# Batch 0's first q and k by two hardware DMA queues, v and w_in triggered anew, its second phase held back, and batch 1's x transposed by DMA

## The chip, the cores and the metric

The kernel runs on one core of one Trainium2 chip, in one launch. The time is device microseconds of that core, from start to end of an execution. The kernel before was timed three times (343.29, 343.39, 343.57: median 343.39 us). One more execution was profiled.

## The reference

Causal attention with 16 extra "beacon" keys and values per head, and behind it a feed-forward layer with a squared ReLU, all without residuals:

```python
B, H, S, Nb, D = 8, 8, 576, 16, 64
k_all = concat([beacon_k, k]); v_all = concat([beacon_v, v])       # 592 keys
scores = q @ k_all.T / sqrt(D)                                     # causal over the 576, beacons always seen
a = softmax(scores)
x = (a @ v_all).transpose(0, 2, 1, 3).reshape(B * S, H * D)        # 4608 tokens x 512
h = x @ w_in                                                       # 512 -> 2048
out = relu(h) ** 2 @ w_out                                         # 2048 -> 512
```

Inputs and output are fp32 in HBM; the kernel computes in bf16 with fp32 accumulation.

## The kernel before

All work is given as small operations to a planner (class `Order`, L89). It holds for each operation the engine, an assumed duration, the operations it depends on and a priority, plays the program through once while the kernel is built, and emits the instructions of every engine in the order that results. On the chip each engine then works through its own list in order and waits on semaphores. So a change of a priority, of an assumed duration or of a limit on PSUM banks moves instructions on all engines. `deps` and `sync` become waits on the chip where data or a buffer is shared (`sync` adds such a wait where nothing is shared); `behind` only shapes the list.

**Attention, per batch and pair of heads** (four pairs per batch, so 32 pairs in all):

- q and k must be transposed. For batches 0 to 2 (`NPE = 3`) this is done on TensorE: `add_strided` (L502) loads q and k with the token index split as 96 partitions x 6, by GpSimd DMAs (L513) that cast fp32 to bf16 on the way. In batch 0 there is one DMA for each pair and each of q and k, eight in all; in batches 1 and 2 one for two pairs. In batches 1 and 2 a copy on VectorE ("spin", L382) brings the two heads of a pair side by side, so that one transpose serves both (L547, 12 per pair); in batch 0 each head is transposed by itself into one half of the PSUM partitions (L550, 24 per pair). Two copies then write kT (VectorE) and qT (ScalarE or VectorE).
- From batch 3 on, q and k are loaded by SP into staging slots (`stg`, eight of them), cast on GpSimd, and transposed by DMA (L459).
- Scores are computed in strips of up to 496 columns (L665), exponentiated on ScalarE (L680), masked on VectorE (L695, L699), multiplied with v (L715), and normalised on VectorE (L730, L731) into `xn`. v is loaded by SP (batch 1: by GpSimd) into `stg` and cast.
- Batch 0 is split into two phases (`NSPLIT = 1`, `SPLIT`): queries 0 to 239 and 240 to 575. The first has one score strip per pair, the second three.

**From xn to the MLP.** The MLP needs x transposed (`xT`). For batches 0 and 1 (`NXPE = 2`) this is done on TensorE (`add_xt_pe`, transposes at L779, copies on ScalarE or VectorE); later batches use five DMA transposes on SP (`add_xt`, L762).

**MLP.** Nine chunks of 512 tokens (`add_chunk`): first layer L843 with relu (L860 on ScalarE, L862 on VectorE) and square (L869), second layer L880, copies to `osb`, stores by SP. Chunk 0 is cut at token 240, where the first phase of batch 0 ends; chunk 1 needs rows of batch 1.

**The order of loads at the start.** GpSimd issues batch 0's eight q/k loads, the triangle mask, the casts of the first two v tiles, then w_in in four quarters (L804), batch 1's q/k, batch 1's v and w_out in four quarters (L813). SP loads the beacon keys (L475), then waits for the first q (`sync`) before it loads batch 0's five v tiles (L426, L427); w_in's first quarter waits for the third v tile (`sync`); batch 2's v, next on SP, waits for the last quarter of w_out (`sync`).

PSUM has eight banks. Classes of operations have limits on how many they may hold: score strips 6 (`strip`), AV 4, MLP 4, transposes 2 (`tp`).

Of the kernel before, what the change touches and what calls it, by code (L numbers as in the profile page):

```python
# [9 lines left out]
FP32 = mybir.dt.float32  # L10
# [78 lines left out]
class Order:  # L89
# [6 lines left out]
    START = {"PE": 0.0, "ACT": 1.5, "DVE": 0.7, "POOL": 0.5, "SP": 0.0, "-": 0.0}  # L96
# [16 lines left out]
    def run(self):  # L113
# [19 lines left out]
        lanes = {"SP": [], "POOL": []}  # L133
# [6 lines left out]
        while events:  # L140
# [16 lines left out]
            while again:  # L157
                again = False
                for e in engines:
# [58 lines left out]
                    if op.dma:  # L218
                        dma_free = max(dma_free, now + (0.65 if e == "SP" else 0.55 + 0.4 * op.dma)) + op.dma
# [34 lines left out]
def kernel(  # L254
# [80 lines left out]
    def wait_for(later, first):  # L335
# [5 lines left out]
        limits={"strip": 6, "av": 4, "mlp": 4, "tp": 2},  # L341
# [7 lines left out]
    nc.scalar.activation(warm, warm, AF.Exp)  # L349
# [20 lines left out]
    ident_op = add("ident", "POOL", 0.6, lambda e: make_identity(nc, ident), prio=-199.8)  # L370
# [28 lines left out]
    NXPE = 2  # L399
# [11 lines left out]
    def add_load(b, x, c, prio, behind=[], sync=[]):  # L411
# [34 lines left out]
        if x != "v":  # L446
            if b < NPE + 2:
                deps += [zero_ops[b]]
            else:
# [3 lines left out]
                            prio=prio, deps=deps, give=ld)  # L453
# [14 lines left out]

    tpb_ops = {}
# [32 lines left out]
    def add_strided(b, prio):  # L502
# [6 lines left out]
        for pr in range(0, HP, step):  # L509
            h = slice(2 * pr, 2 * (pr + step))  # L510
            for n, (x, t, dst) in enumerate((("k", k, ks), ("q", q, qs))):
                def emit(e, t=t, dst=dst, h=h):
# [3 lines left out]
                        deps=free, dma=0.87 * step if b else 1.12)  # L516
# [4 lines left out]
        for pr in range(HP):  # L521
# [11 lines left out]
            if b:  # L533
                for x, t in (("k", ks), ("q", qs)):
                    def emit_spin(e, h=h, x=x, t=t, blocks=blocks):
                        copy_on(e, blocks[x].rearrange("p s (h d) -> p h s d", h=2), t[b % 2][:, h])

                    spin[x].append(add(f"spin{b}{x}{pr}", "DVE", 0.45, emit_spin, prio=prio + pr,
                                       deps=[loads[pr, x]] + spin[x][-1:] + ([tps[b - 1, 0]] if pr == 0 and b > 1 else [])))

            def emit_tp(e, pr=pr, h=h, box=box, blocks=blocks):
                pp = pair(box["t"]).bitcast(BF16)
                for half, at, x, t in ((1, Nb, "k", ks), (0, 0, "q", qs)):
                    for u in range(NS):
                        cols = slice(at + u * NP, at + (u + 1) * NP)
                        if b:
# [8 lines left out]
                     deps=([spin["k"][pr], spin["q"][pr]] if b else [loads[pr, "k"], loads[pr, "q"]]) + [ident_op] + busy,  # L555
                     take=("ps", "tp", [2]), mode="full" if b else "columns")
# [89 lines left out]
    def add_scores(pairs, n, sizes):  # L646
# [4 lines left out]
        for size in sizes:  # L651
# [7 lines left out]
            def emit_qk(e, group=group, box=box):  # L659
                for k, (x, _, (mms, _, _)) in enumerate(group):  # L660
                    st = pair(box["qk"], k)
                    for c, t0, t1, col in mms:
# [11 lines left out]
                     take=("ps", "strip", [2] * size), gate=owners[0].gate, mode="rows")  # L674
# [125 lines left out]
    def add_weights():  # L800
        for i in range(4):
# [5 lines left out]
            w_ops["in", i] = add(f"win{i}", "POOL", 1.3, emit, prio=-100 + i, sync=[v_loads[0][2]] if i == 0 else (),  # L807
                                 behind=[w_ops["in", i - 1]] if i else (), dma=2.6)
    def add_weights_out():
        for i in range(4):  # L810
# [5 lines left out]
            w_ops["out", i] = add(f"wout{i}", "POOL", 1.3, emit, prio=-90 + i, behind=[v_loads[1][4]] if i == 0 else [w_ops["out", i - 1]], dma=2.6)  # L816
# [103 lines left out]
    for b in range(B):  # L920
# [76 lines left out]
```

## Time and profile before

| | |
|---|---|
| median of three runs | 343.39 us |
| profiled execution | 342.96 us |
| its span | 341.1 us |
| TensorE (PE) busy | 325.8 us |
| ScalarE (ACT) busy | 199.9 us |
| VectorE (DVE) busy | 156.5 us |
| GpSimd (POOL) busy | 84.4 us |

How to read the rows that follow. A row of groups or of the timeline has the start, the duration, the engine, the source line, the operation, what it writes and reads with sizes, and in square brackets the idle time before it and who ended that. A row of the stage table has the stretch and its length, then for PE, PEld (weight loads), DVE, ACT and POOL the busy time and the number of instructions, then the granted TensorE clock (1.00 is full), the mean busy share of the 16 DMA engines (above 1 where transfers overlap) and GB/s moved. A row of a tile's or line's instructions has the shortest, middle and longest duration in ns. In the DMA view, the last number of a row is the median time from issue to landing in us; the size is that of the destination.

### The profile page before, as it was taken

Reading aid. Unit: us, or ns where it says so; the run is one execution under the profiler, and the core shown is the slowest. Engines: PE = TensorE matmul, PEld = TensorE weight load, DVE = VectorE, ACT = ScalarE, POOL = GpSimd, SP = SyncE. Lnnn points to the kernel's source line nnn. Section 1 sums busy time; section 2 is a strip of 40 time slices with the busy share of each in tenths; the row PEclk is TensorE's granted clock in tenths of the full one; section 3 lists DMA queues with packets and bytes.
Section 4 is the critical chain, followed back from the end, with each engine's and each line's share of the span. In section 5 each row is a group of like instructions: output and inputs, shape, how many; then the busy total and the mean of one; then the engine's idle time right before and its main releaser. Section 6 shows DMA issues by size and latency. Waiting matters only on the chain.

```text
span 341.1 us, 7065 instructions
## 1 busy us (share of the span) xinstructions
PE 325.8 (96%) x2844; PEld 177.1 (52%) x2884; DVE 156.5 (46%) x313; ACT 199.9 (59%) x311; POOL 84.4 (25%) x133
## 2 busy tenths in 40 slices
PE   3899999999999999999999999999999999999995
PEld 2568765545455535543556865435544444444442
DVE  5576974569533655247523862267404202301400
ACT  3977977497747775558454755597326326515611
POOL 8364730466350231504151522200000000000000
PEclk9969999999999999999999999999999999999999
DMA  7999999999997996999799989930051011011002
GB/s 96 190 184 204 220 205 215 224 230 208 211 180 163 198 222 110 205 240 241 144 200 224 239 143 211 251 73 1 2 131 63 0 61 63 0 61 63 0 28 95
DMA packets 137008, 49.45 MB, mean 145 GB/s; under 512 B 123344, under 2 KB 132048, under 8 KB 136976
## 3 DMA queue, kind: packets, MB, share of 16 engines
q1 hardware_dynamic: 127184, 40.02, 59.4%
q0 software_dynamic: 9792, 8.98, 16.4%
q8 instruction: 22, 0.36, 0.5%
q14 instruction: 10, 0.08, 0.1%
HBM read 37.22 MB, written 9.44 MB: 137 GB/s over the span
## 4 chain that ended last, share of the span: by engine, by line
PE 90%; DMA 3%; ACT 3%; DVE 1%; issue 1%; POOL 0%; DVEq 0%; ACTq 0%; POOLq 0%
PE ps L880 36%; PE ps L843 35%; PE ps L715 9%; PE ps L665 8%; DMA kT<-qk_area 2%; ACT pt L680 2%; DMA qk_area<-in_q_dram 1%; PE ps L547 1%; PE ps L779 1%; ACT qT L380 1%; PE ps L550 1%; DVE g L862 0%; DVE xn L731 0%; DVE g L869 0%; ACT osb L380 0%
## 5 line engine op out<-in xcount | busy, mean ns | idle before, releaser
L843 PE MATMUL ps<-xT,w_in 128*128 128x512 bf16 (+3 forms) x687 | 133.4, 340 | 1.2 <-DVE g L862 0.3
L880 PE MATMUL ps<-w_out,g 128*128 128x512 bf16 x553 | 128.1, 379 | 1.6 <-issue 0.6
L680 ACT ACTIVATE pt<-ps 128x832 bf16<-128x832 f32 (+4 forms) x128 | 102.9, 874 | 19.1 <-PE ps L665 19.0
L843 PEld LDWEIGHTS <-w_in 128*128 128x128 bf16 x704 | 65.3, 98 | 56.5 <-issue 7.2
L860 ACT ACTIVATE g<-ps 128x512 bf16<-128x512 f32 (+2 forms) x125 | 69.6, 557 | 39.1 <-PE ps L843 38.2
L869 DVE TENSOR_TENSOR g<-g 128x1024 bf16<-128x1024 bf16 (+2 forms) x80 | 53.2, 666 | 79.4 <-ACT g L860 78.2
L880 PEld LDWEIGHTS <-g 128*128 128x128 bf16 x576 | 53.9, 98 | 63.3 <-issue 2.5
L380 ACT COPY osb<-ps 128x512 f32<-128x512 f32 x36 | 21.2, 589 | 67.1 <-PE ps L880 65.7
L382 POOL CAST qk_area<-stg 128x512 bf16<-128x512 f32 (+2 forms) x50 | 33.3, 676 | 55.5 <-DMA stg<-in_k_dram 30.3
L695 DVE TENSOR_TENSOR pt<-pt,tri 128x1024 bf16<-128x1024 bf16 (+1 forms) x36 | 24.9, 694 | 36.5 <-ACT pt L680 36.5
L382 POOL CAST vb<-stg 128x512 bf16<-128x512 f32 (+1 forms) x37 | 25.3, 695 | 61.3 <-DMA stg<-in_v_dram 42.0
L715 PEld LDWEIGHTS <-pt 128*128 128x128 bf16 (+1 forms) x960 | 34.8, 99 | 7.4 <-issue 1.4
L715 PE MATMUL ps<-vb,pt 128*128 128x65 bf16 (+1 forms) x960 | 36.2, 196 | 0.9 <-ACT pt L680 0.7
L665 PE MATMUL ps<-qT,kT 64*128 64x80 bf16 (+6 forms) x400 | 34.3, 290 | 2.2 <-ACT pt L680 0.9
L862 DVE TENSOR_SCALAR g<-ps 128x512 bf16<-128x512 f32 (+2 forms) x35 | 21.8, 626 | 13.8 <-PE ps L843 13.6
L731 DVE TENSOR_TENSOR xn<-ps,rcp 128x640 bf16<-128x640 f32 (+2 forms) x36 | 27.0, 751 | 1.3
L665 PEld LDWEIGHTS <-kT 64*128 64x128 bf16 x400 | 14.2, 98 | 22.7 <-issue 17.5
L730 DVE RECIPROCAL rcp<-ps 128x10 f32<-128x10 f32 (+2 forms) x36 | 7.6, 211 | 33.2 <-PE ps L715 29.8
L380 ACT COPY qT<-ps 128x576 bf16<-128x576 bf16 x12 | 7.8, 653 | 8.2 <-PE ps L550 4.8
L382 DVE COPY kT<-ps 128x576 bf16<-128x576 bf16 x12 | 9.0, 751 | 2.3 <-PE ps L550 1.4
L699 DVE TENSOR_TENSOR pt<-pt,tri 80x160 bf16<-80x160 bf16 x32 | 9.0, 281 | 0.0
L380 ACT COPY xT<-ps 128x576 bf16<-128x576 bf16 (+2 forms) x8 | 4.2, 519 | 3.6 <-PE ps L779 3.6
(43 smaller groups left out, 69.3 us busy)
## 6 DMA issues: line engine op xcount, KB each, us to landing
out_dram<-osb SPq DMA_DIRECT2D x17, 512.0 KB, 3.3
stg<-in_v_dram SPq DMA_DIRECT2D x21, 256.0 KB, 5.4
stg<-in_q_dram SPq DMA_DIRECT2D x20, 256.0 KB, 5.4
stg<-in_k_dram SPq DMA_DIRECT2D x15, 256.0 KB, 4.4
w_in<-in_moe_w_in_dram POOLq DMA_DIRECT2D x4, 512.0 KB, 8.1
w_out<-in_moe_w_out_dram POOLq DMA_DIRECT2D x4, 512.0 KB, 10.8
stg<-in_v_dram SPq DMA_DIRECT2D x7, 224.0 KB, 4.2
qk_area<-in_k_dram POOLq DMA_DIRECT2D x4, 288.0 KB, 12.2
```

The lines of the kernel that those rows point to most:

```text
L380: nc.scalar.copy(dst, src)
L382: eng[e].tensor_copy(dst, src)
L665: nc.tensor.matmul(st[:, hj, col:col + t1 - t0], kT[x.b % 2][hp, x.pr, 128 * c:128 * c + 128], qT[x.b % 2][hp, x.pr, t0:t1], start=True, s ...
L680: nc.scalar.activation(pt[x.take_pt.held[0]][:, :, off:off + width], pair(box["qk"], k)[:, :, 0:width], AF.Exp, bias=0.0, scale=scale)
L695: nc.vector.tensor_tensor(out=d, in0=d, in1=tri[:, m0:m0 + m, :][:, None].to_broadcast([128, 2, m, 128]), op=ALU.min)
L715: nc.tensor.matmul(a[:, hj, (t - tl[0]) * (D + 1):(t - tl[0] + 1) * (D + 1)], P[0:rr, hj, o:o + 128], vb[b % 2][0:rr, c, h, :], start=(c = ...
L731: nc.vector.tensor_tensor(out=xn[b % 2].rearrange("p t (h d) -> p h t d", d=D)[:, 2 * pr:2 * pr + 2, tl[0]:tl[0] + nt], in0=a[:, :, :, 0:D ...
L843: nc.tensor.matmul(h[:, lo - spans[0][0]:hi - spans[0][0]], w_in_sb[:, mc, ft * 128:(ft + 1) * 128], xT[:, mc, lo % RING:lo % RING + hi - lo],
L860: nc.scalar.activation(dst, h, AF.Relu, bias=0.0, scale=1.0)
L862: nc.vector.tensor_scalar(out=dst, in0=h, scalar1=0.0, scalar2=None, op0=ALU.max)
L869: nc.vector.tensor_tensor(out=d, in0=d, in1=d, op=ALU.mult)
L880: nc.tensor.matmul(o, G[:, fc, ts * 128:(ts + 1) * 128], w_out_sb[:, fc, :], start=(fc == 0), stop=(fc == NFT - 1))
```

## The change

- The first pair's q and k of batch 0 are loaded as fp32 by two hardware queues, k on SP and q on ScalarE's, into memory borrowed from `g[1]` (`first`). Copies on VectorE or ScalarE cast and turn them (`spin`), so that this pair takes 12 transposes instead of 24. The remaining six q/k loads of batch 0 stay on GpSimd.
- The load of the exp table moves behind ScalarE's DMA issue; the identity's memset moves from GpSimd to VectorE.
- v of batch 0 waits for the third pair's q (`strided[0][HP - 2, "q"]`) instead of the first pair's; w_in waits for the second v tile instead of the third; batch 2's v no longer waits for w_out (`behind` in place of `sync`, which is an order of the planner and no wait on the chip).
- Casts of batch 0's v tiles 2 to 4 get a later priority.
- Score strips of batch 0's second phase get a class of PSUM banks of their own (`late`, at most 4), transposes may hold 4 banks instead of 2.
- Batch 1's x is transposed by DMA on SP (`NXPE = 1`).
- Assumed durations of the planner: loads of q/k in batch 0 0.76 us instead of 1.12, issue of weights 0.95 instead of 1.3, ScalarE ready at 0.

The built program's lists show what the planner makes of it. TensorE before: pair 0's transposes and first strip, pair 1's transposes, pair 0's second-phase strips, pair 2's transposes and so on; after: transposes of pair 0, transposes of pair 1, first strip of pair 0, transposes of pair 2, first strip of pair 1, transposes of pair 3, first strip of pair 2, then the first second-phase strips of pair 0, then the four AVs of the first phase with the transposes of their results and strips of pairs 0 and 1 between them, and the first MLP matmul before the second phase of pairs 2 and 3 and before any second-phase AV. Batch 1's attention is also placed further ahead: all its score strips but one come before the first second-layer matmul of chunk 0. From chunk 2's first layer on TensorE's list is the same as before. On SP the five DMA transposes of batch 1's x stand ahead of all of batch 3's loads but one, and batch 2's first three v tiles directly behind batch 0's v.

```diff
-    START = {"PE": 0.0, "ACT": 1.5, "DVE": 0.7, "POOL": 0.5, "SP": 0.0, "-": 0.0}
+    START = {"PE": 0.0, "ACT": 0.0, "DVE": 0.7, "POOL": 0.5, "SP": 0.0, "-": 0.0}
...
-        limits={"strip": 6, "av": 4, "mlp": 4, "tp": 2},
+        limits={"late": 4, "strip": 6, "av": 4, "mlp": 4, "tp": 4},
...
-    nc.scalar.activation(warm, warm, AF.Exp)
...
+    nc.vector.memset(ident, 0.0)
+    nc.vector.memset(bks, 0.0)
     nc.vector.memset(tri, BIG)
-    nc.vector.memset(bks, 0.0)
...
-    ident_op = add("ident", "POOL", 0.6, lambda e: make_identity(nc, ident), prio=-199.8)
+    ident_op = add("ident", "POOL", 0.3, lambda e: make_identity(nc, ident, nomemset=True), prio=-198.85)
...
-    NXPE = 2
+    NXPE = 1
...
         cast[b, x, c] = add(f"cast{b}{x}{c}", engs, {"DVE": 0.6, "POOL": 0.65}, emit_cast,
-                            prio=prio, deps=deps, give=ld)
+                            prio=prio + (900.0 if b == 0 and c > 1 else 0.0), deps=deps, give=ld)
...
+    first = {x: g[1][0:NP].rearrange("p f t -> p (f t)")[:, 1536 * i:1536 * (i + 1)].bitcast(FP32).rearrange(
+        "p (h s d) -> p h s d", h=2, s=NS) for i, x in enumerate("kq")}
...
+        if b == 0:
+            add("table", "ACT", 1.5, lambda e: nc.scalar.activation(warm, warm, AF.Exp), prio=prio)
+        for n, (x, t) in enumerate((("k", k), ("q", q)) if b == 0 else ()):
+            def emit(e, t=t, x=x):
+                queue = nc.sync if e == "SP" else nc.scalar
+                return [queue.dma_start(out=first[x], in_=t[0, 0:2].rearrange("h (p s) d -> p h s d", s=NS))]
+
+            loads[0, x] = add(f"sld{b}{x}0", "SP" if n == 0 else "ACT", 0.5, emit, prio=prio - 1 + 0.1 * n, dma=0.76)
-        for pr in range(0, HP, step):
+        for pr in range(1 if b == 0 else 0, HP, step):
...
-                        deps=free, dma=0.87 * step if b else 1.12)
+                        deps=free, dma=0.87 * step if b else 0.76)
...
-            if b:
+            turned = b > 0 or pr == 0
+            if turned:
                 for x, t in (("k", ks), ("q", qs)):
                     def emit_spin(e, h=h, x=x, t=t, blocks=blocks):
-                        copy_on(e, blocks[x].rearrange("p s (h d) -> p h s d", h=2), t[b % 2][:, h])
+                        copy_on(e, blocks[x].rearrange("p s (h d) -> p h s d", h=2), t[b % 2][:, h] if b else first[x])
...
-                     take=("ps", "strip", [2] * size), gate=owners[0].gate, mode="rows")
+                     take=("ps", "late" if b < NSPLIT and n else "strip", [2] * size), gate=owners[0].gate, mode="rows")
...
-            w_ops["in", i] = add(f"win{i}", "POOL", 1.3, emit, prio=-100 + i, sync=[v_loads[0][2]] if i == 0 else (),
+            w_ops["in", i] = add(f"win{i}", "POOL", 0.95, emit, prio=-100 + i, sync=[v_loads[0][1]] if i == 0 else (),
...
-                    sync = [strided[0][0, "q"]]
+                    sync = [strided[0][HP - 2, "q"]]
...
             elif b == 2 and n == 0:
-                sync = [w_ops["out", 3]]
+                behind = [w_ops["out", 3]]
```

More of the change, by code (lines that the diff above doesn't have):

```diff
@@ L132, in run @@
         dma_free = 0.0
-        lanes = {"SP": [], "POOL": []}
+        lanes = {"SP": [], "POOL": [], "ACT": []}
         events = [(t, 0, None, None) for t in sorted(set(free.values()) | {0.0})]
@@ L218, in run @@
                     if op.dma:
-                        dma_free = max(dma_free, now + (0.65 if e == "SP" else 0.55 + 0.4 * op.dma)) + op.dma
+                        dma_free = max(dma_free, now + (0.65 if e != "POOL" else 0.55 + 0.4 * op.dma)) + op.dma
                         seen = max(end, dma_free + 1.4)
@@ L554, in add_strided @@
             tp = add(f"tp{b}.{pr}", "PE", 0.55 if b else 1.0, emit_tp, prio=100.0 * (HP * b + pr) - 190,
-                     deps=([spin["k"][pr], spin["q"][pr]] if b else [loads[pr, "k"], loads[pr, "q"]]) + [ident_op] + busy,
-                     take=("ps", "tp", [2]), mode="full" if b else "columns")
+                     deps=([spin["k"][pr], spin["q"][pr]] if turned else [loads[pr, "k"], loads[pr, "q"]]) + [ident_op] + busy,
+                     take=("ps", "tp", [2]), mode="full" if turned else "columns")
             tps[b, pr] = tp
@@ L815, in emit @@
                     in_=moe_w_out.rearrange("(c p) f -> p c f", p=128)[:, i * n:(i + 1) * n, :])]
-            w_ops["out", i] = add(f"wout{i}", "POOL", 1.3, emit, prio=-90 + i, behind=[v_loads[1][4]] if i == 0 else [w_ops["out", i - 1]], dma=2.6)
+            w_ops["out", i] = add(f"wout{i}", "POOL", 0.95, emit, prio=-90 + i, behind=[v_loads[1][4]] if i == 0 else [w_ops["out", i - 1]], dma=2.6)
     def add_chunk(j):
```

9 lines of the change are left out of this document (5 added, 4 removed).

## The prediction

> **What bounds the kernel now.** I read the page first: its row of engines and its slices.
>
> ```profile
> PE 325.8 (96%) x2844; PEld 177.1 (52%) x2884; DVE 156.5 (46%) x313; ACT 199.9 (59%) x311; POOL 84.4 (25%) x133
> ...
> PE   3899999999999999999999999999999999999995
> ...
> DMA  7999999999997996999799989930051011011002
> ```
>
> TensorE is busy throughout, except in the first slices and at the very end. The table of stages says how much is missing where.
>
> ```profile
> 0.00:5.00 5.00, 0.79 (x16) 0.69 (x16) 3.65 (x21) 1.49 (x2) 3.76 (x11) 1.00 0.47 64
> 5.00:10.00 5.00, 3.33 (x54) 2.37 (x52) 1.83 (x3) 2.28 (x4) 3.06 (x8) 1.00 1.16 152
> ...
> 12.50:15.90 3.40, 2.21 (x46) 1.44 (x43) 1.63 (x3) 3.40 (x6) 1.49 (x3) 1.00 1.26 216
> 15.90:19.30 3.40, 2.99 (x32) 1.78 (x31) 3.19 (x11) 2.92 (x5) 3.40 (x6) 0.50 0.59 89
> 19.30:22.70 3.40, 3.05 (x46) 2.50 (x43) 2.16 (x9) 2.67 (x5) 2.56 (x5) 0.50 1.23 205
> ...
> 24.70:48.00 23.30, 22.54 (x279) 17.83 (x278) 19.99 (x50) 19.59 (x40) 13.62 (x19) 1.00 1.22 211
> ...
> 72.00:336.00 264.00, 261.45 (x2038) 133.09 (x2071) 108.99 (x186) 148.00 (x225) 50.56 (x76) 1.00 0.67 132
> ```
>
> From 24.7 us on TensorE lacks 0.8 us up to 48 and 1% of the rest: what is computed there cannot be hidden, only removed. Before 24.7 it is idle for about 8 us, and the DMA engines are full (share above 1) from 5 to 15.9 and again from 18: the start waits for data. So a change at the start is worth the sum of four things: when dense work begins, how much attention is then still owed, at which clock it runs, and what TensorE work disappears.
>
> The clock needs a second look. The granted clock reads 1.00 up to 15.9, 0.50 up to 22.7, then 1.00. The same 24 transposes of one pair say otherwise for the beginning:
>
> ```profile
> 10.23 1.17 PE L550 MATMUL ps<-ident,qk_area 96*64 96x96 bf16 x24
> ...
> 12.61 0.70 PE L550 MATMUL ps<-ident,qk_area 96*64 96x96 bf16 x24
> ```
>
> 1.17 against 0.70 us: the array is already slow before about 12.5, fast for 3.4 us, slow again for 6.8 us, and fast once the work is dense.
>
> The chain of the start:
>
> ```profile
> 5.18 0.63 POOL L513 DMA_DIRECT2D qk_area<-in_q_dram  x1
> ...
> 8.04 0.78 ACT L680 ACTIVATE pt<-ps 128x736 bf16<-128x736 f32 x1 [0.58 <-PE ps L665]
> ...
> 15.64 3.00 POOL L804 DMA_DIRECT2D w_in<-in_moe_w_in_dram  x4 [1.01 <-DMA stg<-in_v_dram]
> ...
> 24.29 0.35 PE L665 MATMUL ps<-qT,kT 64*128 64x336 bf16 x4
> ...
> 24.74 0.57 PE L843 MATMUL ps<-xT,w_in 128*128 128x240 bf16 x4
> ...
> 25.72 0.32 PE L779 MATMUL ps<-ident,xn 128*128 128x128 bf16 x3 [0.41 <-DVE xn L731]
> ...
> 26.70 0.90 PE L715 MATMUL ps<-vb,pt 128*128 128x65 bf16 x24
> ```
>
> The first exp starts at 8.04, w_in is asked for at 15.64 (after the third v tile), and the first MLP matmul, the start of dense work, runs at 24.74.
>
> **The change part by part.** First the loads of q and k. They take, from issue to landing (answers of the DMA view for one issue each: batch 0's first k, its third q, batch 0's first v tile, the first quarter of w_in, batch 1's first q and second k):
>
> ```profile
> qk_area<-in_k_dram POOLq DMA_DIRECT2D x1, 144.0 KB, 3.0
> ...
> qk_area<-in_q_dram POOLq DMA_DIRECT2D x1, 144.0 KB, 5.2
> ...
> stg<-in_v_dram SPq DMA_DIRECT2D x1, 224.0 KB, 6.5
> ...
> w_in<-in_moe_w_in_dram POOLq DMA_DIRECT2D x1, 512.0 KB, 5.5
> ...
> qk_area<-in_q_dram POOLq DMA_DIRECT2D x1, 288.0 KB, 12.7
> ...
> qk_area<-in_k_dram POOLq DMA_DIRECT2D x1, 288.0 KB, 13.5
> ```
>
> The first k was issued at 1.36 and landed at 4.4; the third q landed at 5.18 + 5.2 = 10.4: five loads later, 1.2 us each, the last of them beside v. The pair on the hardware queues can be issued at 0.8 us instead of 1.36 and 2.11. No such load is in the trace; its landing lies between 1.9 us (below, the 32 KB beacon on SP) and 5.4 us (page, 256 KB of v in the busy stage) after issue; I take 3.2 us, nearer the short one because nothing else runs yet: 4.0. ACT also spends its issue there, and its table load (1.28 us) then still ends by 2.8, before the data.
>
> ```profile
> 0.80 0.40 SPq L475 DMA_DIRECT2D stg<-in_beacon_k_dram  x1
> ...
> stg<-in_beacon_k_dram SPq DMA_DIRECT2D x1, 32.0 KB, 1.9
> ...
> 0.80 1.28 ACT L349 ACT_TABLE_LOAD   x1 [0.80 <-PEq L981]
> ...
> L382 DVE CAST vb<-stg x3: 429/514/637, 15.1 to 18.3; 128x512 bf16<-128x512 f32 x2, 80x512 bf16<-80x512 f32 x1
> ```
>
> The new fp32-to-bf16 turn copies have 768 columns; a cast of 512 takes 0.43 to 0.64, so 0.65 to 0.95 each, on DVE and ACT in parallel. They end near 5.0. But the order built for TensorE now puts the second pair's transposes, which wait for GpSimd's first two loads, ahead of the first score strip. Those are issued as early as the old first pair, yet share the engines with 576 KB of fp32: about 6.2. So the first exp starts near 8.0, as before: the pair's head start buys nothing by itself.
>
> The remaining four GpSimd loads at 1.1 us each (the 1.2 above without v) put the third q at 8.4, 2 us earlier, and the fourth at 10.6. v is now triggered by the third q instead of the first:
>
> ```profile
> 6.43 7.16 SPq L427 DMA_DIRECT2D stg<-in_v_dram  x5
> ...
> 14.02 0.62 POOL L382 CAST vb<-stg 128x512 bf16<-128x512 f32 x1 [0.37 <-DMA stg<-in_v_dram]
> ...
> 16.00:17.00 1.00, 0.78 (x8) 0.46 (x7) 0.96 (x4) 1.00 (x3) 1.00 (x2) 0.50 0.14 21
> 17.00:18.00 1.00, 0.92 (x11) 0.55 (x11) 0.97 (x4) 1.00 (x2) 1.00 (x3) 0.50 0.25 18
> ```
>
> The second v tile was cast at 14.02, 7.6 us after v's first issue; the first k of the kernel took 3.0, and one tile of v more takes about 1.2. Between 4.2 and 7.6 after the trigger I take 5.0, since only two other loads are left beside it: 13.4 instead of 13.9. w_in follows the second v tile instead of the third: 13.5 instead of 15.64, and its first quarter lands at 19.0 instead of 21.1. This also closes the hole of the last two rows, in which the DMA engines ran at a share of 0.14 and 0.25.
>
> The second phase (queries 240 and up) of batch 0 gets its own class of banks, and the order now runs all four first phases before most second ones. From the landed v (13.4) to the first MLP matmul the new order holds, one behind the other, a cast of 0.5, four short AVs, four norms, transposes, xT copies and four score strips. With the slow strips and AVs (0.5 each) that makes 6.5 us, with fast ones (0.35) 4.7. Start of dense work: between 19.0 (w_in) and 19.9; I take **19.4, 5.3 us earlier than 24.7**.
>
> What is still owed then: before, one AV group and two groups of transposes were behind the first MLP matmul; now three more AV groups (0.90 each), two more transposes (0.32) and six score strips (0.35 alone, half of that in a stream, so 0.27): 2.7 + 0.6 + 1.6 = **4.9 us more**.
>
> The clock: TensorE in the changed order is sparse from 12 to 19.4 and so slow at 19.4. If it comes back at 22.7 as now, 3.3 us of dense work run at 0.70/1.17 of full rate: **1.3 us lost**.
>
> Batch 1's xT by DMA transposes removes 20 matmuls of TensorE and four ACT copies of 0.64 us.
>
> ```profile
> 40.00:75.00 35.00, 1.69 (x20) 1.44 (x20) 1.00 1.16 219
> ...
> L762 SPq DMA_TRANSPOSE xT<-xn x30: 1186/1264/2203, 96.8 to 251.9; - x30
> ...
> 68.74 1.90 PE L843 MATMUL ps<-xT,w_in 128*128 128x512 bf16 x8
> ...
> 61.80 5.65 SPq L427 DMA_DIRECT2D stg<-in_q_dram  x4
> ...
> 77.89 4.20 SPq L459 DMA_TRANSPOSE qT<-qk_area  x1
> ```
>
> The first row is these transposes alone: **1.7 us gone**. Their cover: the five DMA transposes take 5 times 1.3 to 2.2 us on SP after the last norm of batch 1 and must be there when chunk 1 begins (68.74 now). In the new order ten groups of four second-layer matmuls (the last row has eight of the first layer in 1.90) and four groups of transposes (0.70) stand between, about 12 us against 7 to 11. If that cover is gone, it costs up to 3 us. Batch 3's q, behind them on SP, moves from 61.80 to about 67; its own transposes are issued at 77.89 now, and TensorE has chunks 1 and 2 to work on until they land: nothing, and up to 5 us if the gap closes.
>
> The last edit drops batch 2's wait for w_out:
>
> ```profile
> SPq L426 <- DMA w_out<-in_moe_w_out_dram: 37.8, 1, 37.8
> ```
>
> Three v tiles (768 KB) that now go at 51 will go as soon as their slots are free, near 17 to 20, beside w_in and batch 1's q and k: bounded by nothing (they overlap) and 768 KB at the 205 GB/s of 19.3 to 22.7, 3.7 us of delay. Batch 1's second k now lands at 20.47 + 13.5 = 34.0; 2.1 us of earlier trigger and half of the delay nearly cancel, so I take zero here. The memsets moved to DVE, the planner's constants and the casts put behind cost nothing that the v wait does not hide.
>
> Sum: -5.3 + 4.9 + 1.3 - 1.7 = **-0.8 us**. The profiled execution took 342.96 (span 341.1 and 1.9 around it), the median is 0.4 above it; the forecast is 343.39 - 0.8 = **342.6**.
>
> **Rivals.**
>
> *Loads at their later speed (faster).* Batch 1's second k landed 1.5 us after its first q (19.80 + 12.7 and 20.47 + 13.5): 0.75 us for each 144 KB, not 1.1. The two to the third q then save 0.7 us, the first four together 1.4, and with less in front of v 1.8; dense work begins at 17.6: 340.8. For it: the slow figure was taken with v alongside. Against: the loads of 4.4 to 9 us, without v, were no faster.
>
> *Dropped wait (slower).* The 768 KB go ahead of w_in's last quarter and batch 1's q and k, which come 3.7 - 2.1 = 1.6 us later than now, while TensorE reaches them no later than now. The copies that turn them stand in DVE's queue ahead of norms and squares, and DVE has no room there (19.99 of 23.3 us now, and the new order gives it six more relus of 0.4 and the four late norms and masks): 1.6 us of waiting, and the squares behind it hold up TensorE for as long again, so 343.4 - 0.8 + 3.2 = 345.8, and 344.6 where 1.2 us of it is hidden, which I take. It decides as soon as batch 1's second k lands after about 36 (34.0 now).
>
> *One more slow stretch.* If the sparse start keeps the array slow for another 3.4 us, that loses 1.4 us more: 344.0, no measurable change. For it: after 15.9 the array needed two such stretches, though it was busy 2.99 of 3.40 us in the first. By the Trainium skill (TensorE: Matmul & The Clock Gate, "What's actually happening") the gate looks at free-running windows of 3.4 us; the trace agrees, 15.9 to 22.7 being two of them.
>
> *The change doesn't do what it says.* The two hardware loads only split one stream, and w_in is not earlier: dense work at 20.4 and 343.6. The Trainium skill (DMA: Bandwidth & Descriptors, "Issuing engines are not separate DMA queues") says that all issuing engines feed the same 16 DMA engines and that a second one saves only issue time; the share of 0.47 in the first 5 us leaves idle engines to fill, so the trace supports it only from 5 us on.
>
> **How the numbers follow.** Forecast 0.37 (its own range 341.8 to 343.3), faster loads 0.18, dropped wait 0.28, slow stretch 0.10, no earlier w_in 0.07. 0.2% is 0.69 us and about what can be told from no change: faster is below 342.7, slower above 344.1. Faster: 0.24 of the forecast and 0.18, together 0.42; slower: 0.27, 0.04 of the slow stretch and 0.03 of the last, 0.34; same: the rest, 0.24. The range takes in 340.8 less a little and the dropped wait with most of its 345.8: 340.4 to 345.4.
>
> **What would show it.** Right: the first MLP matmul between 19.0 and 19.9, w_in's issue near 13.5, the third q landed near 8.4, the first exp near 8, 1.69 us less under the transposes of xn, the granted clock at 1.00 from about 22.7. The dropped wait shows as waits of DVE's or TensorE's on qk_area or w_in between 25 and 40, and as more than 0.8 us of idle TensorE from there to 48. Wrong altogether: dense work after 21, or chunk 1's first matmul waiting for xT's DMA.

## The result, and the profile after

The changed kernel takes 349.44 us (median of four; the kernel before, beside it, 343.48): 1.016 times as long, 95% interval 1.0131 to 1.0189. The forecast was 342.6, and the time lies outside its range. The profiled execution took 349.52 us, its span 347.8. The changed file has 12 lines more ahead of the code in question, so L843 of before is L855, L665 is L677, L715 is L727, L762 is L774. The experiments' own additions move lines by up to 12 more.

The page of the changed kernel, engines and slices:

```profile
PE 327.2 (94%) x2813; PEld 177.1 (51%) x2852; DVE 160.8 (46%) x324; ACT 194.9 (56%) x300; POOL 81.9 (24%) x129
...
PE   2887999999999979999999999999999999999995
...
PEclk9969899999999999999999999999999999999999
```

TensorE has 31 matmuls fewer in the records and is yet 1.4 us longer busy: some of its work ran at a lower clock. Each matmul has a weight load of its own (PEld; in e8 below, whose records are complete, there are 2884 of each), so about 40 matmul records are missing both here (2813 against 2852) and before (2844 against 2884); idle times of the two can be compared with each other, but each is somewhat too long. Idle time is 20.6 us (347.8 less 327.2), 5.3 more than before. The stage table says where:

```profile
15.90:19.30 3.40, 2.47 (x27) 1.05 (x26) 2.43 (x10) 3.31 (x5) 3.33 (x6) 0.65 1.11 178
19.30:22.70 3.40, 2.53 (x19) 1.53 (x20) 1.40 (x5) 1.57 (x4) 0.67 (x1) 0.50 1.23 201
22.70:24.70 2.00, 2.00 (x49) 1.88 (x46) 1.19 (x4) 0.23 (x1) 0.54 (x1) 0.74 1.21 195
24.70:48.00 23.30, 21.15 (x256) 15.99 (x252) 18.21 (x48) 17.43 (x32) 12.80 (x18) 0.93 1.21 204
72.00:336.00 264.00, 259.42 (x2032) 132.29 (x2066) 111.59 (x189) 149.68 (x226) 48.34 (x74) 1.00 0.68 139
...
34.00:36.00 2.00, 2.00 (x29) 1.82 (x28) 1.55 (x6) 0.37 (x1) 1.23 (x3) 0.50 1.27 191
36.00:38.00 2.00, 2.00 (x22) 1.65 (x20) 0.88 (x3) 1.03 (x3) 0.89 (x2) 0.65 1.27 218
```

Two stretches that were dense are dense no longer. From 24.7 to 48 us 2.15 us are idle instead of 0.8, and the clock is 0.93 on average instead of 1.00; the last two rows show it at 0.50 and 0.65 just after a stall. From 72 us on 4.6 us are idle instead of 2.6. (The rest of the 5.3 is 1.35 more up to 24.7 us and 0.4 from 48 to 72.) The list of TensorE's waits names both (us in total, times, longest):

```profile
PE ps L677 <- DMA kT<-qk_area: 2.3, 2, 2.1
PE ps L490 <- DMA bks<-in_beacon_k_dram: 2.0, 1, 2.0
PE ps L855 <- DMA w_in<-in_moe_w_in_dram: 1.6, 1, 1.6
```

The third row is the start of dense work. Here is that start in the timeline:

```profile
9.02 5.41 SPq L427 DMA_DIRECT2D stg<-in_v_dram  x5
9.39 0.79 ACT L692 ACTIVATE pt<-ps 128x736 bf16<-128x736 f32 x1
...
13.68 3.00 POOL L816 DMA_DIRECT2D w_in<-in_moe_w_in_dram  x4 [0.71 <-DMA stg<-in_v_dram]
...
20.17 0.98 PE L855 MATMUL ps<-xT,w_in 128*128 128x240 bf16 x4 [1.63 <-DMA w_in<-in_moe_w_in_dram]
```

Dense work begins at 20.17 instead of 24.74: this half of the forecast came about, nearly as sized (4.6 us earlier, not 5.3). What follows did not. The first stall is for batch 1's beacon keys, `bks`, at 31 us:

```profile
17.43 6.75 SPq L427 DMA_DIRECT2D stg<-in_v_dram  x3
...
33.42 0.26 PE L490 MATMUL ps<-ident,bks 128*128 128x16 bf16 x4 [1.98 <-DMA bks<-in_beacon_k_dram]
...
33.71 0.23 DVE L494 CAST kT<-ps 128x64 bf16<-128x64 f32 x1 [2.10 <-PE ps L490]
33.85 0.45 DVE L382 COPY sparek<-qk_area 96x768 bf16<-96x768 bf16 x1
```

VectorE's queue stood behind it for 2.10 us, the copies that turn batch 1's first keys with it. `bks` is 16 KB and was issued at 17.31; it took this long (answers of the DMA view for one issue each, first before, then after: `bks`, batch 1's second k, first quarter of w_in; last `bks` in experiment e1, the changed kernel with the wait put back):

```profile
bks<-in_beacon_k_dram POOLq DMA_DIRECT2D x1, 16.0 KB, 11.9
```

```profile
bks<-in_beacon_k_dram POOLq DMA_DIRECT2D x1, 16.0 KB, 16.1
...
qk_area<-in_k_dram POOLq DMA_DIRECT2D x1, 288.0 KB, 19.0
...
w_in<-in_moe_w_in_dram POOLq DMA_DIRECT2D x1, 512.0 KB, 6.4
```

```profile
bks<-in_beacon_k_dram POOLq DMA_DIRECT2D x1, 16.0 KB, 12.2
```

In the kernel before it was issued at 19.27, landed at 31.2 and was read at 32.02, with nothing to wait for. Now it is issued 2 us earlier and lands 2.2 us later. Beside it run three tiles of batch 2's v, which SP sends from 17 us on since it no longer waits for w_out (the row at 17.43); with these held back and the same lists (e1) it takes 12.2 us again. The second stall is 90 us later; SP's timeline leads to it:

```profile
63.36 7.41 SPq L774 DMA_TRANSPOSE xT<-xn  x5
70.88 0.52 SPq L427 DMA_DIRECT2D stg<-in_q_dram  x1
...
84.57 5.39 SPq L459 DMA_TRANSPOSE qT<-qk_area  x1
...
121.05 4.02 SPq L459 DMA_TRANSPOSE kT<-qk_area  x1
...
127.95 0.76 PE L677 MATMUL ps<-qT,kT 64*128 64x496 bf16 x8 [2.11 <-DMA kT<-qk_area]
```

Batch 3's first q is loaded at 70.88 instead of 61.80, its transpose is issued at 84.57 instead of 77.89, and batch 4's k is transposed at 121.05. In the kernel before, with a wait for `kT` of 0.3 us at 121.6, this row was:

```profile
113.57 6.03 SPq L459 DMA_TRANSPOSE kT<-qk_area  x1
```

### The profile page after: what moved, and what is told of

It is laid out like the page before. It is cut to its first block, busy times and chain, and to the rows that moved or that the text cites. A ratio compares the mean times of both kernels' runs of the same rounds, so it can differ in the third digit from the quotient of the medians.

```text
span 347.8 us, 7025 instructions
## 1 busy us (share of the span) xinstructions
PE 327.2 (94%) x2813; PEld 177.1 (51%) x2852; DVE 160.8 (46%) x324; ACT 194.9 (56%) x300; POOL 81.9 (24%) x129
## 4 chain that ended last, share of the span: by engine, by line
PE 74%; DMA 14%; SPq 3%; ACT 2%; POOL 2%; issue 2%; DVE 2%; POOLq 0%; ACTq 0%; DVEq 0%
PE ps L892 32%; PE ps L855 30%; PE ps L727 6%; PE ps L677 6%; DMA bks<-in_beacon_k_dram 5%; DMA kT<-qk_area 4%; DMA stg<-in_v_dram 2%; DMA stg<-in_k_dram 2%; SPq L774 2%; DMA qk_area<-in_q_dram 1%; ACT pt L692 1%; PE ps L559 1%; POOL w_in L816 1%; SPq L427 1%; POOL qk_area L523 1%
## 5 line engine op out<-in xcount | busy, mean ns | idle before, releaser
L855 PE MATMUL ps<-xT,w_in 128*128 128x512 bf16 (+3 forms) x688 | 135.8, 343 | 2.4 <-DMA w_in<-in_moe_w_in_dram 1.6
L855 PEld LDWEIGHTS <-w_in 128*128 128x128 bf16 x704 | 65.8, 99 | 60.9 <-issue 8.1
L872 ACT ACTIVATE g<-ps 128x512 bf16<-128x512 f32 (+2 forms) x117 | 66.3, 567 | 41.0 <-PE ps L855 40.1
L382 POOL CAST qk_area<-stg 128x512 bf16<-128x512 f32 (+2 forms) x50 | 32.2, 647 | 59.0 <-DMA stg<-in_q_dram 41.5
L382 POOL CAST vb<-stg 128x512 bf16<-128x512 f32 (+1 forms) x36 | 24.6, 692 | 64.8 <-DMA stg<-in_v_dram 59.9
L707 DVE TENSOR_TENSOR pt<-pt,tri 128x1024 bf16<-128x1024 bf16 (+1 forms) x36 | 24.3, 678 | 31.3 <-ACT pt L692 31.2
L727 PEld LDWEIGHTS <-pt 128*128 128x128 bf16 (+1 forms) x960 | 34.8, 99 | 6.7 <-issue 1.0
L677 PE MATMUL ps<-qT,kT 64*128 64x80 bf16 (+7 forms) x400 | 34.0, 287 | 3.2 <-DMA kT<-qk_area 2.3
L727 PE MATMUL ps<-vb,pt 128*128 128x65 bf16 (+1 forms) x960 | 36.2, 196 | 0.4 <-DVE vb L382 0.3
L874 DVE TENSOR_SCALAR g<-ps 128x512 bf16<-128x512 f32 (+2 forms) x43 | 25.7, 602 | 19.3 <-PE ps L855 19.0
L677 PEld LDWEIGHTS <-kT 64*128 64x128 bf16 x400 | 13.7, 96 | 22.8 <-issue 14.9
L711 DVE TENSOR_TENSOR pt<-pt,tri 80x160 bf16<-80x160 bf16 x32 | 10.3, 321 | 0.0
L559 PE MATMUL ps<-ident,sparek 96*128 96x96 bf16 x18 | 1.5, 229 | 6.1 <-ACT sparek L380 6.1
```

The costliest lines, as they stand in the source:

```text
L382: eng[e].tensor_copy(dst, src)
L677: nc.tensor.matmul(st[:, hj, col:col + t1 - t0], kT[x.b % 2][hp, x.pr, 128 * c:128 * c + 128], qT[x.b % 2][hp, x.pr, t0:t1], start=True, s ...
L707: nc.vector.tensor_tensor(out=d, in0=d, in1=tri[:, m0:m0 + m, :][:, None].to_broadcast([128, 2, m, 128]), op=ALU.min)
L727: nc.tensor.matmul(a[:, hj, (t - tl[0]) * (D + 1):(t - tl[0] + 1) * (D + 1)], P[0:rr, hj, o:o + 128], vb[b % 2][0:rr, c, h, :], start=(c = ...
L855: nc.tensor.matmul(h[:, lo - spans[0][0]:hi - spans[0][0]], w_in_sb[:, mc, ft * 128:(ft + 1) * 128], xT[:, mc, lo % RING:lo % RING + hi - lo],
L872: nc.scalar.activation(dst, h, AF.Relu, bias=0.0, scale=1.0)
```

## The experiments

The theory after the result: the start itself is near neutral; batch 2's free v delays batch 1's beacon keys, q and k; the DMA transposes of batch 1's x delay batch 3's and 4's loads on SP. Its rival: the new order of the start is the loss, and the two waits only show it. Ratios are to the kernel before, timed beside each experiment.

**Each later part undone in the changed kernel, and done alone in the kernel before.** `hold` is a wait on the chip that the planner doesn't see, and `quiet` drops one, so that every engine's list stays as it was.

```diff
 e1_v_waits (changed kernel)
+            if b == 2 and n == 0:
+                load_chain[-1].hold = [w_ops["out", 3]]
 e2_x_on_pe (changed kernel)
-    NXPE = 1
+    NXPE = 2
 e3_before_v_free (kernel before)
+            load_chain[-1].quiet = b == 2 and n == 0
 e4_before_x_by_dma (kernel before)
-    NXPE = 2
+    NXPE = 1
```

> The changed kernel, same order on every engine, but batch 2's first v load waits on the chip for the last quarter of w_out again. Theory A (the 768 KB of freed v take DMA time from w_in and from batch 1's q, k and beacon loads): the beacon load of batch 1 lands within 12 us of its issue instead of 16.1, the 2.0 us wait of TensorE for it at 31.4 is gone, and with it the half clock from 33 to 37 (1.5 to 2 us); 345.0 to 346.5. Theory B (that load is late because GpSimd's own chain of loads is full, v is not in its way): the wait stays, 349.

> The changed kernel with batch 1's x on TensorE again (the planner's order shifts with it). Theory A (five DMA transposes on SP hold back batches 3 and 4's loads, and the 2.1 us wait for kT at 126 comes from that): the kT wait is gone or under 0.5 us, TensorE has 1.7 us more to do; 348.5 to 350. Theory B (the kT wait comes from the late start alone): the wait stays and the time is 350.5 to 351.5.

> The kernel before, same order on every engine, only batch 2's first v load no longer waits for w_out on the chip. Theory A (freed v takes DMA time from w_in and batch 1's loads): batch 1's second q lands 3 to 5 us later than 36.1, TensorE waits for it; 345.0 to 347.5. Theory B (v fits beside them): 343.0 to 344.0.

> The kernel before with batch 1's x by DMA transposes and nothing else (the planner's order shifts with it). Theory A (the transposes on SP cost later what they save on TensorE): 1.7 us less of TensorE work, given back as waits for xT or kT, 343.0 to 345.0. Theory B (they are covered): 341.5 to 342.2.

| | median us | ratio to before |
|---|---|---|
| changed kernel | 349.44 | 1.0160 (1.0131 to 1.0189) |
| e1, v waits again | 346.21 | 1.0072 (1.0050 to 1.0094) |
| e2, x on TensorE again | 348.06 | 1.0126 (1.0099 to 1.0152) |
| e3, before with v free | 350.82 | 1.0184 (1.0146 to 1.0222) |
| e4, before with x by DMA | 350.70 | 1.0189 (1.0140 to 1.0238) |

With the wait back, the changed kernel is 0.9% faster, with the same lists. Its waits no longer name `bks`, and its clock stays up at 34 to 38 us; the wait for `kT` is still there. Stage table and waits of e1:

```profile
24.70:48.00 23.30, 22.90 (x329) 17.65 (x328) 21.36 (x56) 20.14 (x39) 13.82 (x19) 1.00 1.23 210
...
34.00:36.00 2.00, 1.94 (x24) 1.47 (x25) 2.00 (x6) 1.74 (x4) 2.00 (x3) 1.00 1.07 223
```

```profile
PE ps L678 <- DMA kT<-qk_area: 2.3, 1, 2.3
```

Dropping that one wait in the kernel before costs 1.8%, and TensorE's timeline has the same stall, longer (first row, e3). e4 shows the other stall (second row), and in its stage table a low clock after it:

```profile
36.02 0.26 PE L489 MATMUL ps<-ident,bks 128*128 128x16 bf16 x4 [2.50 <-DMA bks<-in_beacon_k_dram]
```

```profile
126.94 0.76 PE L665 MATMUL ps<-qT,kT 64*128 64x496 bf16 x8 [3.47 <-DMA kT<-qk_area]
```

```profile
128.00:130.00 2.00, 1.90 (x6) 0.73 (x5) 0.69 (x1) 2.00 (x3) 0.62 (x1) 0.50 1.27 243
```

So in the kernel before as in the changed one, each of the two parts brings its stall with it. Both alone cost more than expected (345 to 347.5 and 343 to 345), and more than in the changed kernel; in e4 the planner also reshapes other lists, so its whole loss is not the transposes'.

e2 says that the stall on `bks` is not the only form that the loss takes. There v is still free, and the wait for `kT` is gone, as theory A had it, but so is the wait for `bks`: in its lists TensorE comes to it only at 33.05, when it has landed (17.4 + 15.2). The kernel is yet 1.3% slower than before. Its trace shows the free v in another place, at batch 0's last v tile:

```profile
22.66 0.42 DVE L382 CAST vb<-stg 80x512 bf16<-80x512 f32 x1 [3.94 <-DMA stg<-in_v_dram]
```

TensorE waits 1.15 us for a mask behind it. With the same lists and batch 2's v waiting (e5, below) this tile is cast at 18.49, and VectorE does not wait for it.

**The new start alone, and its triggers alone.** e5 undoes both later parts at once. e8 is the kernel before with only the two triggers (here `hold` takes the place of the wait).

```diff
 e5_front_alone (e1)
-    NXPE = 1
+    NXPE = 2
 e8_before_triggers (kernel before)
+        w_ops["in", 0].hold = [v_loads[0][1]]
...
+                load_chain[-1].hold = [strided[0][2, "q"]]
```

> The changed kernel with both later parts undone: batch 2's v waits again on chip for w_out's last quarter, and batch 1's x is transposed on TensorE again. What is left is the new start of batch 0 (two hardware loads, triggers, second phase held back). Theory A (three parts add up): 346.21 (v waits again) less the 1.4 that transposing on TensorE alone gave back, 344.8, between 344.3 and 345.3; so the start alone costs 0.8 to 1.8 against the kernel before; no wait for bks or kT over 0.5 us. Theory B (the start is the gain that the prediction's sum would leave once half clock and owed attention are smaller, and the loss is all in the two later parts): 342.0 to 343.3. Theory C (the start itself is the larger loss): above 345.5.

> The kernel before, same lists on every engine, with only the two triggers of the change: batch 0's v waits for the third pair's q instead of the first pair's, w_in for the second v tile instead of the third. Theory A (the prediction's: data for the first MLP matmul come earlier and its list has no room for it): the third q lands near 9.5 instead of 10.4, v's second tile no earlier than 14, w_in issued 1 to 1.5 us earlier, the first MLP matmul moves by less than 0.7 us, time 343.0 to 343.8. Theory B (closing the hole in the DMA engines' use at 16 to 18 us is a gain): 341.8 to 342.8. Theory C (a later v is paid at once, TensorE waits for vb): 344.2 to 346.

e5: 344.62 us against 344.06, 1.0017 (1.0002 to 1.0032). No wait of TensorE's for the DMA of `bks` or `kT` is left, and its stage table is full from 72 us on. (This trace lacks no matmul record, 2073 beside 2071 weight loads, so its 0.08 us of idle time is not to be set against the 2.6 of the kernel before; e8 below, which has the lists of the kernel before and all records, is 0.9 us idle there.)

```profile
72.00:336.00 264.00, 263.92 (x2073) 133.40 (x2071) 112.31 (x189) 148.45 (x225) 45.61 (x68) 1.00 0.65 132
```

This is the verdict between theory and rival: of the 1.60% the start has 0.17, x by DMA 0.55 (e1 less e5), the dropped wait 0.88 (changed kernel less e1). By the other way over e2 the shares are 0.34 for x and 1.09 for the wait; in both the start has the least, though the 0.34 has an interval of about 0.4 to either side and is not clear of the start's 0.17. Since `NXPE` changes the planner's order, what is called x by DMA takes in the lists that come with it.

e8: 344.65 us, 1.0013 (1.0001 to 1.0025). The triggers by themselves bring nothing forward, since without the hardware loads v goes out only at 10.36, when the third q has landed; w_in even goes out 0.35 us later than before:

```profile
10.36 4.66 SPq L428 DMA_DIRECT2D stg<-in_v_dram  x5
...
15.99 3.00 POOL L805 DMA_DIRECT2D w_in<-in_moe_w_in_dram  x4
```

Theory A of e8 had w_in 1 to 1.5 us earlier: wrong. Nearest is theory C: the time lies in its range, and TensorE waits 0.8 us for `vb`, which the list of the kernel before does not have. The loss of 0.13% is too small to give to one wait.

**What batch 2's v must stay clear of.** e10 lets it go once batch 1's last q load has landed, beside w_out. e12 leaves it free and only issues the beacon load ahead of w_in.

```diff
 e10_v_after_qk (e1)
-                load_chain[-1].hold = [w_ops["out", 3]]
+                load_chain[-1].hold = [strided[1][HP - 1, "q"]]
 e12_beacon_first (changed kernel)
+        self.ahead(issued, ("bkl1",), "win0")
```

> The changed kernel, same lists, with batch 2's first v waiting on chip for batch 1's last q load instead of for w_out's last quarter (or nothing). Theory A (the dropped wait costs because 768 KB of v run beside w_in and batch 1's q and k): as good as with the wait for w_out, 345.6 to 346.8, no wait for bks, the wait for kT of 2 us stays. Theory B (v must also stay clear of w_out and batch 1's v): 347.5 to 349.4.

> The changed kernel with batch 2's v free as in the change, and only batch 1's beacon load moved ahead of w_in's first quarter on GpSimd (it stands behind w_in and batch 1's first k). Theory A (the stall on the beacon keys is itself the loss of the dropped wait): no wait for bks, 347.2 to 348.2, against 349.44. Theory B (batch 1's q and k behind it are as late, so the stall only moves to their copies or transposes): waits on qk_area or sparek of 1 us or more at 31 to 40, 348.6 to 349.8.

e10: 346.69 us, 1.0090 (1.0064 to 1.0116), no wait for `bks`. Within the intervals that is e1: here v may run beside w_out, but not beside w_in and batch 1's q and k. e12: 348.38 us, 1.0138 (1.0102 to 1.0175), between the ranges of its two theories. The stall on the beacon is gone; TensorE then waits for a copy that turns one of batch 1's later pairs:

```profile
43.02 0.43 PE L567 MATMUL ps<-ident,qk_area 96*128 96x96 bf16 x6 [1.06 <-DVE qk_area L390]
```

That is a wait of the kind that theory B named, a little later than the 31 to 40 us it gave. But VectorE itself waits only 0.8 us for batch 1's q from 24 to 46 us, so that the beacon keys were the first of several late loads is not shown. The intervals of e12 and the changed kernel overlap, so how much the move brings stays open.

**Why kT is late.** e6 moves the DMA transposes on SP behind the loads that follow; e7 takes them off SP; e11 puts five of batch 3's loads ahead of them; e13 joins the last two and also puts a sixth load ahead of chunk 0's stores.

```diff
 e6_xt_behind (e1)
+        self.after_load(issued, "xt1.", "s1.1.0.0")
+        self.after_load(issued, "xt2.", "ld4k4")
 e7_xt_on_act (e1)
+                queue = nc.scalar if b == 1 else nc.sync
 e11_v_qk_loads_ahead (e10)
+        self.ahead(issued, ("ld3q0", "ld3q1", "ld3q2", "ld3q3", "ld3k1"), "xt1.0")
 e13_act_loads_ahead (e7), besides the line of e11
+        self.ahead(issued, ("st0.0",), "ld3k2")
+        self.ahead(issued, ("st0.1",), "ld3k4")
```

`after_load` and `ahead` place the named operations directly ahead of the last-named one in the list that is emitted.

> The changed kernel with batch 2's v waiting again, and batch 1's five DMA transposes moved on SP behind three of batch 3's q loads and a store, batch 2's five behind all of batch 4's q and k loads, as in the kernel before. Same lists on the other engines. Theory A (SP's list is a chain without slack from batch 3's loads to batch 4's transposes, and five transposes lengthen it by 7 us wherever they stand): batch 4's k is transposed at 115 to 117 again, TensorE waits 1.5 to 2.5 us for kT, time 345.6 to 346.8 (346.21 without the move). Theory B (their place ahead of the loads is what costs): k transposed near 113.5, wait for kT below 0.6, time 343.8 to 344.8. Under either, chunk 1 may now wait for xT, which would show as TensorE waiting for DMA of xT near 68 to 75 and add up to 3 us.

> The changed kernel with batch 2's v waiting again, and batch 1's five DMA transposes issued by ScalarE's queue instead of SP's. Theory A (SP's list is the chain): SP has its 7 us back, batch 4's k is transposed by 113, TensorE's wait for kT falls from 2.3 us to below 0.6, and time is 343.8 to 344.6 as far as ScalarE's exps are not held up. Theory B (the transposes cost the DMA engines, not SP): kT waits 1.5 us or more again, 345.6 to 346.8. Theory C (ScalarE is held up by five issues of 1.3 us where it makes exps): TensorE waits 2 to 6 us for pt or ps near 60 to 75, 346 to 350.

> The same, and on SP batch 3's first five q/k loads moved ahead of batch 1's five DMA transposes (and so ahead of chunk 0's stores too); lists of the other engines as in the changed kernel. Theory A (what costs is SP's list: batch 3's loads stand behind transposes that wait for the last norm, and behind stores that wait for chunk 0): GpSimd's casts of batch 3 find their data and run in a row near 66, batch 4's k is transposed by 114, the wait for kT is below 0.6 us, time 343.4 to 344.6. Theory B (the transposes' 7 us on SP are too much wherever they stand): kT waits 1.5 us or more, 345.6 to 346.8. Theory C (the transposes then come too late): TensorE waits 1 to 4 us for xT near 68 to 74, 345 to 348.

> The changed kernel with batch 2's v waiting again for w_out, batch 1's five DMA transposes issued by ScalarE's queue, and on SP six of batch 3's q/k loads ahead of chunk 0's stores (in the run with ScalarE's queue alone, SP stood 9 us at chunk 0's first store, from 59.8 to 69.2, with those loads behind it). Theory A (batch 4's k is late because SP's list holds up batch 3's loads, by transposes or by stores alike): GpSimd's casts of batch 3 run in a row from about 66, batch 4's k is transposed by 114, TensorE waits neither for kT nor for xT over 0.6 us, time 344.0 to 345.6, at least 2 us below the 347.99 of that run. Theory B (the five transposes cost as DMA traffic, whichever queue and order): kT waits 1.5 us or more, 346.5 to 348.5.

| | median us | ratio | wait for kT's DMA, us | for xT's DMA, us |
|---|---|---|---|---|
| e1 | 346.21 | 1.0072 | 2.3 | none |
| e6 | 356.40 | 1.0380 | none | 7.2 + 3.2 |
| e7 | 347.99 | 1.0104 | 2.3 | none |
| e11 | 350.35 | 1.0184 | none | 3.2 |
| e13 | 347.51 | 1.0100 | none | none |

e7 had looked like the plain test, and theory A failed in it: SP had its 7 us back, and `kT` was as late. Its SP timeline shows why:

```profile
59.79 0.50 SPq L428 DMA_DIRECT2D stg<-in_q_dram  x1
69.21 0.40 SPq L917 DMA_DIRECT2D out_dram<-osb  x1
```

With the transposes gone, SP stands nearly 9 us at chunk 0's first store, which goes out at 69.21 instead of 58.36, ahead of batch 3's loads but two. Chunk 0's second layer begins at 50.6 in e7 instead of 46.7, because batch 1's attention was placed further ahead (54.5 in the changed kernel, with the delay by v in it). The same store holds SP in e6 before it comes to the transposes, and chunk 1 then waits for them (SP, then TensorE):

```profile
67.56 0.41 SPq L925 DMA_DIRECT2D out_dram<-osb  x1
...
69.69 6.96 SPq L784 DMA_TRANSPOSE xT<-xn  x5
```

```profile
76.64 1.89 PE L865 MATMUL ps<-xT,w_in 128*128 128x512 bf16 x4 [7.21 <-DMA xT<-xn]
```

In e11 and e13 the wait for `kT` is gone. With batch 3's loads ahead, GpSimd's first four casts run in a row (e13, 66.64 to 68.93; in the changed kernel it waits for these loads one by one, up to 3.9 us). But this is not what theory A said, which had batch 4's k transposed by 114. In e11 k lands later than in e10 (126.5 against 125.2), and the wait is gone only because TensorE, held up elsewhere, comes to it 6.5 us later (128.98 instead of 122.45). In e13 k is issued 0.4 us earlier than in e7 and lands 2.2 us earlier (117.16 + 5.9 against 117.55 + 7.7), and TensorE comes 3.4 us later; the rows of e7, then of e13:

```profile
117.55 4.01 SPq L460 DMA_TRANSPOSE kT<-qk_area  x1
125.30 0.86 PE L678 MATMUL ps<-qT,kT 64*128 64x496 bf16 x8 [2.30 <-DMA kT<-qk_area]
```

```profile
117.16 4.00 SPq L470 DMA_TRANSPOSE kT<-qk_area  x1
126.44 0.76 PE L688 MATMUL ps<-qT,kT 64*128 64x496 bf16 x8
```

And neither is fast. e11 waits for xT in its place (first row), and in e13 ScalarE issues the transposes where it should copy chunk 0's output, for which TensorE then waits (second row, from the list of waits):

```profile
73.79 1.86 PE L864 MATMUL ps<-xT,w_in 128*128 128x512 bf16 x4 [3.18 <-DMA xT<-xn]
```

```profile
PE ps L688 <- ACT osb L391: 1.9, 1, 1.9
```

So the runs show that batch 1's x by DMA, with the lists that come with it, makes `kT` late: batch 4's k is transposed at 116.25 in e1 and at 110.99 in e5, at 120.98 in e4 and at 113.57 before. Which link of the chain does it stays open. One that no run takes by itself: in the new list batch 2's five transposes stand ahead of batch 4's last six loads, where in the kernel before one load stands behind them, and in e13 SP waits 4.1 us for batch 2's last norm there. (e6 moves them back too, but its own stalls cover what that brings.) That a better list would bring the time down by 2 us was wrong for each list tried. Of the places tried for the five transposes, none was free: 7 to 8 us of a queue are taken from loads, from stores or from ScalarE. No experiment was faster than the kernel before.

## Why the prediction was wrong

**The start was right in its sum.** The third q was predicted at 8.4 and landed at 8.6 (3.72 + 4.9); w_in's issue 13.5, measured 13.68; first MLP matmul 19.4, measured 20.17, a little outside the 19.0 to 19.9 that it gave (19.11 in e1, with the same lists). Its terms, -5.3 + 4.9 + 1.3, make +0.9 us; e5 measured +0.6, with an interval of 0.1 to 1.1. No run tests the terms singly, and luck may be in the agreement: dense work began 4.6 us earlier, not 5.3, and the clock, which was to be back at 22.7, is still 0.74 on average from there to 24.7. Two more sizes were off: the pair on the hardware queues took 4.4 and 4.7 us to land, not 3.2 ("nothing else runs yet" did not hold, GpSimd's loads run beside it from 1.37 us on), so the first exp starts at 9.39 and not "near 8.0, as before"; and w_in's first quarter took 6.4 us, not 5.5. The second hid the first: TensorE waits 1.63 us for w_in at 20.17, and an earlier exp would not have helped there.

**The dropped wait was the step that failed most:** "2.1 us of earlier trigger and half of the delay nearly cancel, so I take zero here". It costs 0.88%, 3.0 us. Batch 1's beacon and second k did not lose half of 3.7 us but 4.2 us (11.9 to 16.1) and 5.5 us (13.5 to 19.0) from issue to landing, more than the upper bound; against e1, which has the same lists, it is 3.9 (12.2) and 5.3 (13.7). Why more than the bytes account for stays open. And the step asked what the delay does to landing times only; it did not ask what stands behind the first thing that is late. The rival "Dropped wait (slower)" had the sign, the threshold (the second k now lands at 37.5, beyond its 36) and about the size, +3.2 us. It had the wrong place for the changed kernel: not VectorE's queue of copies first, but TensorE's own list, at four tiny matmuls on 16 KB. In e3 the place that it named shows as well, VectorE waits 2.6 us for batch 1's first k there, behind the beacon.

**X by DMA was mis-sized, with the sign.** "1.7 us gone" is true of the work: no transposes of batch 1's xn are left. The cover of chunk 1's xT held too, there is no wait for it. What failed is "nothing, and up to 5 us if the gap closes" for batch 3's loads behind them. The gap was looked for at batch 3; it closed at batch 4. That SP from batch 3's loads on is one chain of loads, casts and transposes is the likely reason, but no run isolates the link. The trace of before had the hint, unquoted: TensorE already waits 0.3 us for batch 4's `kT` there. The net is +0.55%, 1.9 us, in place of -1.7 (over e2 +0.34%, 1.2 us, with an interval that takes in none; -1.7 lies outside both).

**A stall was priced at its length.** The two stalls add up to 4.1 us, and of their two causes the first costs 3.0 us where TensorE waits 2.0. The clock can account for the rest: 0.50 and 0.65 at 34 to 38 us, which at full rate would be about 1.7 us less (an estimate from these rows: half of 2.0, and 0.35 of 2.0), and which is 1.00 in e1. The rival of one more slow stretch had looked for it in the sparse start; it came in dense work, behind a wait.

## What to carry to other kernels

When a wait ahead of loads is dropped, list what shares the DMA engines with them and is read first by the bottleneck engine's own list; a 16 KB load behind larger ones decides as well as a large one. When work moves to a DMA queue, follow that queue to the next point where the bottleneck engine already waits on it, even for 0.3 us, and not only to the next use. In a list made by a planner, stores are part of that queue too: moving a chunk's second layer later moves its stores, and the loads behind them. And when a wait goes away in an experiment, look whether the data came earlier or the reader later, before the cause is called found.

## What the runs showed of the hardware

**A stall of 2 to 3 us in dense work can cost a stretch of half clock on top.** TensorE waits 2.78 us for `kT` in e10 and 3.18 us for xT in e11; the stage tables after it (first e10, then e11, the clock is the third number from the end):

```profile
126.00:128.00 2.00, 1.95 (x6) 0.78 (x8) 0.69 (x1) 2.00 (x3) 0.83 (x2) 0.63 1.34 221
128.00:130.00 2.00, 2.00 (x7) 0.66 (x5) 1.54 (x2) 0.30 (x1) 1.16 (x3) 0.51 1.34 202
```

```profile
74.00:76.00 2.00, 2.00 (x8) 0.43 (x6) 0.31 (x1) 0.00 (x0) 0.00 (x0) 0.50 0.66 227
76.00:78.00 2.00, 2.00 (x8) 0.59 (x5) 0.38 (x1) 1.72 (x2) 0.00 (x0) 0.50 1.00 315
```

It does not always come: behind the 2.11 us at 126 us in the changed kernel and the 2.29 us in e1 the clock stays at 1.00; behind the 2.30 us of e7 at the same place it is 0.50 and 0.69 from 126 to 130 us, and behind the 1.98 us at 31 us of the changed kernel 0.50 and 0.65. The Trainium skill (TensorE: Matmul & The Clock Gate, "What's actually happening") puts the slow state after at least one idle window of about 3.4 us and calls the windows free-running. That a stall of one length has either outcome agrees with the free-running part. The 3.4 us do not fit as a least length of a stall: here 1.98 us without a matmul were followed by half clock. Executions of one kernel with such a stall lie up to 3.7 us apart (344.84 to 348.58 in e1), those of e5, without one, 2.4 us; that the clock makes the whole of this spread was not tested.

**Beside each other, fp32 loads on hardware queues and GpSimd's casting loads took about the same time.** In the changed kernel the first pair's k, loaded as fp32 (288 KB) by SP, took 4.4 us to land, its q 4.7 us on ScalarE's queue. The second pair's k and q, which GpSimd issues at 1.37 and 2.11 us and which are cast on the way to 144 KB, took 4.8 and 4.5 beside them. In the kernel before, without the fp32 loads, GpSimd's first k took 3.0.
